# Elementwise work of the first feed-forward moved from GpSimd to VectorE, and the order of its queues changed

## The chip, the cores and the metric

The kernel runs on one core of a Trainium2 chip. The metric is the device time of one execution in microseconds; lower is better. The engines are TensorE (PE in the rows; its weight loads are PEld), VectorE (DVE), ScalarE (ACT), GpSimd (POOL) and SyncE (SP), whose queue issues the DMAs.

## The reference

Attention over 8 batches of 8 heads, 512 local and 32 global positions, heads of 64. A local query sees the global keys and the local keys at most 32 positions away; a global query sees all keys. The result, 4608 tokens of 512, goes through a feed-forward of 2048 with softplus between two products.

```python
s_g = scale * np.matmul(q_g, k_all.transpose(0, 1, 3, 2))
out_g = np.matmul(sm(s_g), v_all)
s_ll = np.where(np.abs(pos[:, None] - pos[None, :]) <= 32, scale * np.matmul(q_l, k_l.transpose(0, 1, 3, 2)), -1e9)
s_l = np.concatenate([scale * np.matmul(q_l, k_g.transpose(0, 1, 3, 2)), s_ll], axis=-1)
out_l = np.matmul(sm(s_l), np.concatenate([v_g, v_l], axis=2))
...
h = x @ w_in
g = np.maximum(h, 0.0) + np.log1p(np.exp(-np.abs(h)))
out = g @ w_out
```

## The kernel before

**The work.** Heads go in pairs: 32 pairs m, four to a batch, so that a pair fills the 128 partitions. The feed-forward takes one batch b at a time, its 512 local tokens, in 16 tiles f of 128 hidden units (a ninth, shorter round takes the global tokens). Each operand of its products is split into an upper half that TensorE takes at full rate and the rest: x into xh and xl, g into gh and gl, the weights into two halves of one tile. A product is then three matmuls (upper by upper, upper by rest, rest by upper), so h of a tile is 12 matmuls and its part of the output 12.

**Batch 0 (pairs 0 to 3)** is done first, in ten steps of a tight software pipeline (`scores0`, `invert0`, `diag0`, `turn0`, `evict0`, `values0`, `split0` and their global forms, whose names end in g). Here the order on VectorE and ScalarE is written out by hand: `keep("dve", ...)` and `keep("act", ...)` chain each instruction to the one before. `split0` casts the values into xh (ScalarE, L224) and subtracts for xl (VectorE, L226); `split0g` copies the global values into yg (L267). While this goes on, weight tiles are prepared, one to a step (`held`): `abs_w` (ScalarE, L479), four operations on bits in `bits_w` (VectorE, L486, L488, L489, L492), and `halves_w`, which copies the upper half (ScalarE, L497) and subtracts for the lower (GpSimd, L498). There are 32 weight tiles, in the order `order_w`; W_PRE = 12 of them are done in the steps.

**Pairs 4 to 31** go through pieces, each with a due time: scores of three parts p at 12 m + 4 p, values 22 (LAG) later, then `invert` and `normalise` 3 and 6 after the last values. Scores write PSUM (up to pair 7 the mask is added by TensorE, MPE = 8, and ScalarE copies the scores out; later VectorE adds the mask, L315), then a transposing reduction (L316) collects maxima of blocks of 32. After the third part, `maxima` (three copies across partitions on GpSimd, L329, then small reductions and copies on VectorE) and `probs` three times: a transpose spreads the maxima into mb (L347), GpSimd subtracts them (L352, L354, L355), ScalarE takes the exponential (L356). `values` multiplies into PSUM, ScalarE copies the result into x (L369, L373), and VectorE adds the overlapping columns (L374, L375). From pair 6 on, scores and values share one PSUM buffer, "a". `combine` sends the row sums through DRAM, `invert` takes the reciprocal and sends it back as rb, `normalise` multiplies (L404), and `split_x` splits the result for the next batch (L451, L452).

**The feed-forward's items** are half tiles of h (`hpart`) and, two tiles later, half tiles of the output (`opart`): 60 items in batch 0, each of 6 matmuls. After the second half of h comes `act`: Abs, Exp, Ln on ScalarE (L540 to L542), maximum and add on VectorE (e, L543, which frees the PSUM buffer of h; there are two), the cast gh on ScalarE (L546) and the subtraction gl on GpSimd (L547). After each item of batch 0 the weights are prepared up to W_AHEAD + w RATE / 8, where w is 4 f + 2 or 4 f + 4 from f = 1 on, and loaded AHEAD = 4 further; then all pieces go whose due time has come: from START at the first item to `first` + 48 = 120 at the last.

**Order.** TensorE's instructions run in the order in which the program emits them (`mm` chains each to the one before). For the other engines a planner lays out each queue ahead of time by when it expects instructions to be ready, and by emission among those that are ready; `after(i, what)` adds that i comes behind the last instruction noted under that name. So the bits of a weight behind the steps come after the latest maxima (L487). On the chip every queue runs in the order laid out.

Of the kernel before, what the change touches and what calls it, by code (L numbers as in the profile page):

```python
# [8 lines left out]
F32 = mybir.dt.float32  # L9
# [3 lines left out]
AF = mybir.ActivationFunctionType  # L13
ALU = mybir.AluOpType
# [18 lines left out]
LAG = 22  # L33
STEP = 3
GW = 75
W_AHEAD = 9
W_PRE = 12
START = 69
RATE = 4
A_LO = 8  # L40
A_UP = 5
# [12 lines left out]
def moe_over_global_local_attention(  # L54
# [271 lines left out]
    def maxima(m):  # L326
        mt = st.pop(("mt", m))
        for a in range(1, 4):
            nc.gpsimd.tensor_copy(mt[0:32, GW * a:GW * a + GW], mt[32 * a:32 * a + 32, 0:GW])  # L329
        e0 = 4 * GW  # L330
        for u, du, off in ((0, 1, -2), (3, 1, 3)):
            nc.vector.tensor_reduce(grid(mt, e0 + u, (7, 6), (du, 2)), grid(mt, 3 + u, (12, 6), (du, 2), (off, 2), (GW, 4)), axis=AX.XY, op=ALU.max)
        nc.vector.tensor_reduce(grid(mt, e0 + 2, (7, 6), (4, 2)), grid(mt, 3 + 2, (12, 6), (7, 2), (GW, 4)), axis=AX.X, op=ALU.max)
        g = e0 + 44
        nc.vector.tensor_reduce(grid(mt, g, (1, 2)), grid(mt, 3 + 5, (36, 2), (12, 3), (3, 2), (GW, 4)), axis=AX.XYZ, op=ALU.max)
        nc.vector.tensor_copy(grid(mt, e0 + 5, (21, 2), (7, 3)), mt[0:32, g:g + 2].unsqueeze(2).to_broadcast([32, 2, 3]))
        e = mt[:, e0:e0 + 44]
        for a in range(1, 4):
            i = nc.vector.tensor_copy(e[32 * a:32 * a + 32, 0:42], e[0:32, 0:42]).ins
        order["maxima"] = i  # L340
        st["e", m] = e

    def probs(m, p):
        s, e = st["s", m, p], st["e", m]
        k = QW[p] // 32
        mb = pl.tile([P, 2, 288], F32, tag="mb", name=f"mb{m}_{p}", bufs=2)
        nc.vector.transpose(mb[:, :, :QW[p]].rearrange("p h (s k) -> p h s k", k=32),  # L347
                            windows(e, 7 * p, 21, 2, k).unsqueeze(3).to_broadcast([P, 2, k, 32]))
        for h in range(2):
            if p < 2:  # L350
                sw = s[:, h].rearrange("p (c w) -> p c w", w=192)
                nc.gpsimd.tensor_tensor(sw, sw, windows(mb[:, h], 0, 96, 2, 192), op=ALU.subtract)  # L352
        if p == 2:
            nc.gpsimd.tensor_tensor(s[:, :, 0:192], s[:, :, 0:192], mb[:, :, 0:192], op=ALU.subtract)  # L354
            nc.gpsimd.tensor_tensor(s[:, :, 192:288], s[:, :, 192:288], mb[:, :, 96:192], op=ALU.subtract)  # L355
        nc.scalar.activation(s, s, AF.Exp, scale=0.125)  # L356

    def values(m, p):
        s, vt = st.pop(("s", m, p)), st["v", m]
# [51 lines left out]
    def pieces():  # L411
# [6 lines left out]
        for m in range(M0, M):  # L418
            for p in range(NPC):
                fs = [lambda m=m, p=p: scores(m, p)]  # L420
                if m + 1 < M:
                    fs.append(lambda m=m, p=p: load(m + 1, p))
                if p == 2:
                    fs.append(lambda m=m: maxima(m))
                    fs += [lambda m=m, q=q: probs(m, q) for q in range(NPC)]
                ps.append((12 * m + 4 * p, piece(*fs)))
                fs = [lambda m=m, p=p: values(m, p)]
                if p == 2:
                    fs.append(lambda m=m: combine(m))
                    if m + 2 < M:  # L430
                        fs.append(lambda m=m: load_v(m + 2))
                    ps.append((end(m) + STEP, lambda m=m: invert(m)))
                    ps.append((end(m) + 2 * STEP, lambda m=m: normalise(m)))
                ps.append((12 * m + 4 * p + LAG, piece(*fs)))
# [39 lines left out]
    def abs_w(kind, k):  # L474
        if A_LO <= k < NF - A_UP:
            a = pl.tile([P, 512], I32, tag=f"{kind}{k + A_UP}", name=f"wbits{kind}{k}", bufs=1)
        else:
            a = pl.tile([P, 512], I32, tag="mb", name=f"wbits{kind}{k}", bufs=2)
        note("act", nc.scalar.activation(a.bitcast(F32), raws[kind, k][:, :, 1].bitcast(F32), AF.Abs))  # L479
        return a  # L480

    def bits_w(kind, k, a):
# [1 line left out]
        lo32, hi32 = t[:, :, 0], t[:, :, 1]  # L484

        i = nc.vector.tensor_scalar(a.bitcast(F32), a.bitcast(F32), TINY, None, op0=ALU.max)  # L486
        note("dve", i) if tight else after(i, "maxima")  # L487
        note("dve", nc.vector.tensor_scalar(a, a, 3, 0x3FFFFFFF, op0=ALU.logical_shift_left, op1=ALU.bitwise_and))  # L488
        note("dve", nc.vector.scalar_tensor_tensor(a, hi32, -0x40000000, a, op0=ALU.bitwise_and, op1=ALU.bitwise_or))  # L489

# [4 lines left out]
    def halves_w(kind, k, r):  # L495
        (wi if kind == "wi" else wo)[k] = o = pl.tile([P, 2, 512], F32R, tag=f"{kind}{k}", name=f"{kind}{k}", bufs=1)
        note("act", nc.scalar.copy(o[:, 0], r))  # L497
        nc.gpsimd.tensor_tensor(o[:, 1], r, o[:, 0].bitcast(F32), op=ALU.subtract)  # L498

    def split_w(kind, k):  # L500
        halves_w(kind, k, bits_w(kind, k, abs_w(kind, k)))
# [10 lines left out]
    def moe_items():  # L512
# [24 lines left out]
        def act(b, f):  # L537
# [6 lines left out]
            gh = pl.tile([P, 512], F32R, tag="gh", name=f"gh{b}_{f}", bufs=3)  # L544
            gl = pl.tile([P, 512], F32R, tag="gl", name=f"gl{b}_{f}", bufs=3)
            nc.scalar.copy(gh, e)  # L546
            nc.gpsimd.tensor_tensor(gl, e, gh.bitcast(F32), op=ALU.subtract)  # L547
            g[b, f] = (gh, gl)

        def opart(b, f, t):  # L550
# [93 lines left out]
    for k in range(-2, n + 2):  # L644
        stage(k + 2, 0)

        while k >= n - 2 and pcs[0][0] < min(12 * M0 + 8 * (k - n + 3), START):
            pcs.pop(0)[1]()
        if k == 0:
            key_masks()  # L650
        if held:
# [7 lines left out]
        if held:  # L659
            halves_w(*held[:2], r)  # L660
            held = None
        if -1 <= k and wk[1] < W_PRE:
            held = order_w[wk[1]]
            held += (abs_w(*held),)
            wk[1] += 1
# [2 lines left out]
        halves_w(*held[:2], bits_w(*held))  # L668
    items = moe_items()
    loads(W_PRE + 6)  # L670
    weights(W_AHEAD)
    total = [sum(it[1] for it in items if it[0] == b) for b in range(B + 1)]
    gone = [0] * (B + 1)
# [70 lines left out]
```

## Time and profile before

| | |
|---|---|
| time, median of 3 runs | 1098.7 us (1097.0 to 1100.11) |
| the profiled execution | 1099.49 us |
| its span, first to last instruction | 1097.4 us |
| PE busy | 1037.4 us, 95% |
| VectorE busy | 599.2 us, 55% |
| ScalarE busy | 549.8 us, 50% |
| GpSimd busy | 466.7 us, 43% |
| mean granted TensorE clock | 0.977 |

Busy times are unions of the instructions of an engine. Shares over the span are means over stages that differ: batch 0's attention, the first feed-forward together with the preparation of weights, then seven feed-forwards with the attention of the pairs ahead beside them.

### The profile page before, as it was taken

How to read it: one execution, taken by the hardware profiler on the slowest of the kernel's cores; microseconds unless marked ns; L12 is line 12 of the kernel's file. 1: busy time of each engine (PE TensorE's matmuls, PEld its weight loads, DVE VectorE, ACT ScalarE, POOL GpSimd, SP SyncE). 2: the span in 40 equal slices, each digit the busy share in tenths (PEclk: the TensorE clock that was granted, in tenths of full speed). 3: DMA queues.
4: the chain of work that ended last, by engine and by line, in shares of the span. 5: the costliest groups of instructions: out<-in, count | busy, mean ns of one | idle time of the engine just before them, and what ended most of it. 6: DMA issues, size and time to landing. Idle time of an engine off the chain costs nothing.

```text
span 1097.4 us, 14272 instructions
## 1 busy us (share of the span) xinstructions
PE 1037.4 (95%) x5108; PEld 799.0 (73%) x5108; DVE 599.2 (55%) x1137; ACT 549.8 (50%) x972; POOL 466.7 (43%) x554
## 2 busy tenths in 40 slices
PE   6896788999999999999999999999999999999996
PEld 4674566767777777777777777777777778788895
DVE  5979697874445655565555544565546542311211
ACT  6855555544444544545444544554454544454452
POOL 2136475762345444454444344544445442222221
PEclk9997889999999999999999999999999999999998
DMA  9432332322112212123211312122212210110010
GB/s 359 157 98 86 108 129 64 94 53 84 50 49 49 89 44 55 47 54 93 55 48 52 93 44 55 48 81 53 55 45 55 84 28 13 32 39 1 1 39 20
DMA packets 78566, 74.14 MB, mean 68 GB/s; under 512 B 53380, under 2 KB 57476, under 8 KB 78496
## 3 DMA queue, kind: packets, MB, share of 16 engines
q1 hardware_dynamic: 77952, 73.17, 22.6%
q8 instruction: 40, 0.66, 0.2%
q14 instruction: 30, 0.25, 0.1%
q10 hardware_dynamic: 544, 0.07, 0.0%
HBM read 63.51 MB, written 9.71 MB: 67 GB/s over the span
## 4 chain that ended last, share of the span: by engine, by line
PE 74%; DVE 8%; DMA 4%; issue 3%; POOL 1%; ACT 1%; DVEq 0%; ACTq 0%; SPq 0%; POOLq 0%
PE h L124 30%; PE o L124 30%; PE v_ps L124 9%; PE s_ps L124 5%; DMA rb<-rec_scratch 3%; DVE xa L404 2%; DMA rec_scratch<-sc 1%; DVE xl L452 1%; DVE xh L451 1%; DVE s L315 1%; DVE mb L347 0%; DVE wbitswo L489 0%; DVE woraw L492 0%; DMA raw<-in_qk 0%; DVE wbitswo L486 0%
## 5 line engine op out<-in xcount | busy, mean ns | idle before, releaser
L124 PE MATMUL h<-xh,wi 128*128 128x512 f32 (+1 forms) x1152 | 357.9, 394 | 20.0 <-DVE xl L226 10.3
L124 PE MATMUL o<-wo,gh 128*128 128x512 f32 x1088 | 346.9, 400 | 0.0
L547 POOL TENSOR_TENSOR gl<-e,gh 128x512 fp32r<-128x512 f32 x136 | 178.5, 1313 | 378.9 <-ACT gh L546 322.7
L124 PEld LDWEIGHTS h<-xh,wi 128*128 128x128 f32 x1152 | 208.7, 190 | 69.7 <-issue 17.2
L124 PEld LDWEIGHTS o<-wo,gh 128*128 128x128 f32 x1088 | 201.4, 189 | 47.3 <-issue 4.0
L124 PE MATMUL h<-xl,wi 128*128 128x512 f32 (+1 forms) x576 | 221.1, 384 | 2.8 <-DVE xl L452 2.8
L540 ACT ACTIVATE e<-h 128x512 f32<-128x512 f32 x136 | 81.3, 598 | 272.3 <-PE h L124 265.5
L124 PE MATMUL o<-wo,gl 128*128 128x512 f32 x544 | 213.6, 393 | 0.0
L543 DVE SCALAR_TENSOR_TENSOR e<-h,e 128x512 f32<-128x512 f32 x136 | 93.2, 685 | 182.9 <-ACT e L542 182.9
L352 POOL TENSOR_TENSOR s<-s,mb 128x384 f32<-128x384 f32 x112 | 137.7, 1261 | 14.2 <-DVE mb L347 14.2
L124 PEld LDWEIGHTS h<-xl,wi 128*128 128x128 f32 x576 | 109.6, 190 | 27.7 <-DVE xl L452 5.8
L546 ACT CAST gh<-e 128x512 fp32r<-128x512 f32 x136 | 84.2, 619 | 90.0 <-DVE e L543 90.0
L124 PE MATMUL v_ps<-s,v 128*65 128x192 f32 (+1 forms) x672 | 126.3, 319 | 2.1 <-DVE s L315 1.8
L124 PEld LDWEIGHTS o<-wo,gl 128*128 128x128 f32 x544 | 103.0, 189 | 22.7
L124 PEld LDWEIGHTS v_ps<-s,v 128*65 128x65 f32 (+1 forms) x672 | 85.3, 136 | 41.5 <-issue 15.9
L315 DVE TENSOR_TENSOR s<-s_ps,mask 128x768 f32<-128x768 f32 (+1 forms) x96 | 64.7, 694 | 90.9 <-PE s_ps L124 90.9
L542 ACT ACTIVATE e<-e,one 128x512 f32<-128x512 f32 x136 | 98.5, 724 | 3.3
L356 ACT ACTIVATE s<-s 128x768 f32<-128x768 f32 (+1 forms) x84 | 66.6, 792 | 66.5 <-POOL s L352 51.4
L124 PE MATMUL s_ps<-raw 64*128 64x192 f32 (+1 forms) x672 | 81.8, 350 | 13.5 <-issue 9.4
L541 ACT ACTIVATE e<-e 128x512 f32<-128x512 f32 x136 | 85.6, 630 | 3.4
L124 PEld LDWEIGHTS s_ps<-raw 64*128 64x128 f32 (+1 forms) x672 | 50.2, 181 | 49.8 <-issue 41.3
L316 DVE TRANSPOSE_TENSOR_REDUCE mt<-s 128x24 f32<-128x768 f32 (+1 forms) x84 | 76.2, 908 | 13.4 <-ACT s L312 9.7
(144 smaller groups left out, 839.3 us busy)
## 6 DMA issues: line engine op xcount, KB each, us to landing
raw<-in_qk SPq DMA_DIRECT2D x56, 272.0 KB
v<-in_v SPq DMA_DIRECT2D x28, 384.0 KB
out<-ot SPq DMA_DIRECT2D x34, 256.0 KB
rb<-rec_scratch SPq DMA_DIRECT2D x28, 304.0 KB
wiraw<-in_w_in SPq DMA_DIRECT2D x16, 512.0 KB
woraw<-in_w_out SPq DMA_DIRECT2D x16, 512.0 KB
raw<-in_qk SPq DMA_DIRECT2D x28, 192.0 KB
v<-in_v SPq DMA_DIRECT2D x4, 512.0 KB
```

What stands on the lines that cost most here:

```text
L124: order["pe"] = after(nc.tensor.matmul(*a, **k), "pe").ins
L315: nc.vector.tensor_tensor(s[:n, :, o:o + w], ps[:n, :, o:o + w], mk[:n].unsqueeze(1).to_broadcast([n, 2, w]), op=ALU.add)
L316: order["scores"] = nc.vector.tensor_reduce(windows(mt, 3 + 12 * p, 36, 2, nb), s.rearrange("p h (b k) -> p h b k", k=32), axis=AX.X, op=A ...
L352: nc.gpsimd.tensor_tensor(sw, sw, windows(mb[:, h], 0, 96, 2, 192), op=ALU.subtract)
L356: nc.scalar.activation(s, s, AF.Exp, scale=0.125)
L404: after(nc.vector.tensor_tensor(y[64 * h:64 * h + 64], x[0:64, h], rb[:, h], op=ALU.mult), "scores")
L540: nc.scalar.activation(e, ph, AF.Abs)
L541: nc.scalar.activation(e, e, AF.Exp, scale=-1.0)
L542: nc.scalar.activation(e, e, AF.Ln, bias=one)
L543: nc.vector.scalar_tensor_tensor(e, ph, 0.0, e, op0=ALU.max, op1=ALU.add)
L546: nc.scalar.copy(gh, e)
L547: nc.gpsimd.tensor_tensor(gl, e, gh.bitcast(F32), op=ALU.subtract)
```

## The change

On VectorE instead of GpSimd, for as long as the first feed-forward lasts: the copies in `maxima` and the subtractions in `probs` of pairs 4 to 7 (m < MPE), the lower halves of weight tiles prepared after the steps, and gl of batch 0.

Order: maxima and probs of a pair become a piece of their own, due half a unit after its last scores, and in the steps only whole due times are taken, so those of pairs 4 and 5 are emitted behind all steps. The copies of `maxima` on VectorE and the first operation on bits come behind the last instruction of the steps on VectorE, the exponentials of `probs` and the Abs of later weights behind the last on ScalarE.

Pace: nine weight tiles instead of twelve are prepared in the steps (k from 0 to 8, not from -1 to 10); W_AHEAD is 12 instead of 9, so that three more are emitted straight behind the steps and the later ones three further ahead; START is 64 instead of 69.

```diff
-W_AHEAD = 9
+W_AHEAD = 12
...
-START = 69
+START = 64
...
     def maxima(m):
         mt = st.pop(("mt", m))
         for a in range(1, 4):
-            nc.gpsimd.tensor_copy(mt[0:32, GW * a:GW * a + GW], mt[32 * a:32 * a + 32, 0:GW])
+            if m < MPE:
+                after(nc.vector.tensor_copy(mt[0:32, GW * a:GW * a + GW], mt[32 * a:32 * a + 32, 0:GW]), "dve")
+            else:
+                nc.gpsimd.tensor_copy(mt[0:32, GW * a:GW * a + GW], mt[32 * a:32 * a + 32, 0:GW])
...
+        sub = nc.vector.tensor_tensor if m < MPE else nc.gpsimd.tensor_tensor
...
-                nc.gpsimd.tensor_tensor(sw, sw, windows(mb[:, h], 0, 96, 2, 192), op=ALU.subtract)
+                sub(sw, sw, windows(mb[:, h], 0, 96, 2, 192), op=ALU.subtract)
         if p == 2:
-            nc.gpsimd.tensor_tensor(s[:, :, 0:192], s[:, :, 0:192], mb[:, :, 0:192], op=ALU.subtract)
-            nc.gpsimd.tensor_tensor(s[:, :, 192:288], s[:, :, 192:288], mb[:, :, 96:192], op=ALU.subtract)
-        nc.scalar.activation(s, s, AF.Exp, scale=0.125)
+            sub(s[:, :, 0:192], s[:, :, 0:192], mb[:, :, 0:192], op=ALU.subtract)
+            sub(s[:, :, 192:288], s[:, :, 192:288], mb[:, :, 96:192], op=ALU.subtract)
+        after(nc.scalar.activation(s, s, AF.Exp, scale=0.125), "act")
...
+                ps.append((12 * m + 4 * p, piece(*fs)))
                 if p == 2:
-                    fs.append(lambda m=m: maxima(m))
-                    fs += [lambda m=m, q=q: probs(m, q) for q in range(NPC)]
-                ps.append((12 * m + 4 * p, piece(*fs)))
+                    fs = [lambda m=m: maxima(m)] + [lambda m=m, q=q: probs(m, q) for q in range(NPC)]
+                    ps.append((12 * m + 4 * p + 0.5, piece(*fs)))
...
-        note("act", nc.scalar.activation(a.bitcast(F32), raws[kind, k][:, :, 1].bitcast(F32), AF.Abs))
+        i = nc.scalar.activation(a.bitcast(F32), raws[kind, k][:, :, 1].bitcast(F32), AF.Abs)
+        note("act", i) if tight else after(i, "act")
...
-        note("dve", i) if tight else after(i, "maxima")
+        note("dve", i) if tight else after(after(i, "maxima"), "dve")
...
-        nc.gpsimd.tensor_tensor(o[:, 1], r, o[:, 0].bitcast(F32), op=ALU.subtract)
+        (nc.gpsimd if tight else nc.vector).tensor_tensor(o[:, 1], r, o[:, 0].bitcast(F32), op=ALU.subtract)
...
-            nc.gpsimd.tensor_tensor(gl, e, gh.bitcast(F32), op=ALU.subtract)
+            (nc.gpsimd if b else nc.vector).tensor_tensor(gl, e, gh.bitcast(F32), op=ALU.subtract)
...
-        while k >= n - 2 and pcs[0][0] < min(12 * M0 + 8 * (k - n + 3), START):
-            pcs.pop(0)[1]()
+        if k >= n - 2:
+            for pc in [pc for pc in pcs if pc[0] < min(12 * M0 + 8 * (k - n + 3), first - 2) and pc[0] % 1 == 0]:
+                pcs.remove(pc)
+                pc[1]()
...
-        if -1 <= k and wk[1] < W_PRE:
+        if 0 <= k < n - 1 and wk[1] < W_PRE:
...
     loads(W_PRE + 6)
+    while pcs[0][0] < first - 2:
+        pcs.pop(0)[1]()
     weights(W_AHEAD)
```

## Rows read from the trace of the kernel before

**Rows 1.** Busy us (instructions) of each engine by stretch, granted clock, DMA share, GB/s.

```profile
60.00:80.00 20.00, 20.00 (x149) 14.74 (x147) 16.64 (x34) 10.34 (x21) 6.80 (x10) 1.00 0.36 96
80.30:190.40 110.10, 84.14 (x382) 61.37 (x382) 89.78 (x142) 62.45 (x107) 66.26 (x66) 0.87 0.32 103
190.40:241.50 51.10, 49.21 (x233) 36.95 (x233) 40.55 (x75) 26.06 (x45) 31.26 (x35) 0.94 0.27 74
300.00:400.00 100.00, 98.60 (x483) 75.09 (x483) 59.62 (x114) 49.20 (x81) 49.37 (x60) 1.00 0.23 62
...
190.40:196.90 6.50, 6.41 (x20) 5.00 (x21) 6.43 (x11) 3.57 (x6) 3.17 (x3) 0.52 0.44 120
```

**Rows 2.** Waits of PE, 80 to 250 us: total us, times, longest.

```profile
PE h L124 <- DVE xl L226: 10.3, 1, 10.3
PE s_ps L124 <- issue: 9.4, 2, 6.1
PE s_ps L124 <- ACT wo L497: 4.1, 1, 4.1
PE h L124 <- DVE xh L451: 2.7, 1, 2.7
```

**Rows 3.** Timeline, 76 to 92 us: start us, us, instruction [idle before, releaser].

```profile
78.43 0.60 PE L124 MATMUL o<-p_1gl,v 96*128 96x256 f32 x2
...
83.81 0.72 ACT L224 CAST xh<-o 64x256 fp32r<-64x256 f32 x2
...
90.93 0.85 DVE L226 TENSOR_TENSOR xl<-o,xh 64x256 fp32r<-64x256 f32 x2
...
91.92 0.77 PE L124 MATMUL h<-xh,wi 128*128 128x512 f32 x1 [10.31 <-DVE xl L226]
```

**Rows 4.** Timeline around the second part of pair 8's scores.

```profile
190.18 0.21 DVE L375 TENSOR_TENSOR x<-x,v_ps 65x64 f32<-65x64 f32 x1
...
190.49 1.65 PE L124 MATMUL s_ps<-raw 64*128 64x192 f32 x8 [3.33 <-issue]
```

**Rows 5.** Timeline, 85 to 115 us: operations on weight bits, and a GpSimd subtraction.

```profile
101.53 0.42 DVE L486 TENSOR_SCALAR wbitswo<-wbitswo 128x512 f32<-128x512 f32 x1
...
101.99 0.43 DVE L488 TENSOR_SCALAR wbitswo<-wbitswo 128x512 int32<-128x512 int32 x1
...
104.92 1.50 POOL L547 TENSOR_TENSOR gl<-e,gh 128x512 fp32r<-128x512 f32 x1 [0.20 <-ACT gh L546]
...
105.19 1.52 DVE L486 TENSOR_SCALAR wbitswo<-wbitswo 128x512 f32<-128x512 f32 x1
```

**Rows 6.** Timeline, 12 to 20 us: the Abs of the first weight tile.

```profile
15.12 0.64 ACT L479 ACTIVATE wbitswi<-wiraw 128x512 f32<-128x512 f32 x1
```

**Rows 7.** Groups by line and form on VectorE, 262 to 900 us: busy us, mean ns.

```profile
L347 DVE STREAM_TRANSPOSE mb<-mt 128x576 f32<-128x576 f32 x44 | 31.7, 758 | 0.8
...
L452 DVE TENSOR_TENSOR xl<-xa,xh 128x384 fp32r<-128x384 f32 x10 | 5.3, 528 | 0.0
```

**Rows 8.** Chain that ended last, 260 to 290 us: start us, us, what.

```profile
272.76 2.75 PE h L124 x12
```

**Rows 9.** Busy us by stretch of tile wbitswo's instructions, then wbitswi's: VectorE, ScalarE.

```profile
80.30:190.40 110.10, 28.01 (x34) 5.98 (x9) 0.87 0.32 103
...
80.30:190.40 110.10, 30.73 (x35) 5.95 (x9) 0.87 0.32 103
```

**Rows 10.** Timeline of VectorE at 157 us: two independent operations in a row.

```profile
157.50 0.68 DVE L492 SCALAR_TENSOR_TENSOR wiraw<-wiraw,wbitswi 128x512 int32<-128x512 int32 x1
158.10 0.67 DVE L489 SCALAR_TENSOR_TENSOR wbitswi<-wiraw,wbitswi 128x512 int32<-128x512 int32 x1
```

**Rows 11.** Groups by line and form on GpSimd, 80.3 to 190.4 us.

```profile
L352 POOL TENSOR_TENSOR s<-s,mb 128x384 f32<-128x384 f32 x15 | 16.0, 1089 | 9.4 <-DVE mb L347 9.4
L547 POOL TENSOR_TENSOR gl<-e,gh 128x512 fp32r<-128x512 f32 x10 | 14.6, 1463 | 4.2 <-ACT gh L546 3.7 <-POOL mt L329 0.5
L498 POOL TENSOR_TENSOR wo<-woraw,wo 128x512 fp32r<-128x512 f32 x8 | 14.4, 1797 | 6.0 <-ACT wo L497 6.0
```

## The prediction, made before the changed kernel was run

> **What bounds the kernel now.** I read the windows first, then PE's waits, then the timeline at each wait. From 300 us on PE is busy 98.6 of 100 us, so nothing that this change touches can matter there; between 80.3 and 190.4 it is busy 84 of 110 at a granted clock of 0.87, and that is the stretch of the first feed-forward [rows 1]. Four waits hold most of its loss: 10.3 us in one piece before the first matmul of h, 9.4 in two pieces before scores, 4.1 before another, 2.7 at the change to the second batch [rows 2]. The first is a queue, not work: the last values of batch 0 leave PE at 79.0, but their cast to xh stands behind exponentials on ScalarE until 83.81, and xl, behind weight bits and maxima on VectorE, starts at 90.93 [rows 3]. The waits before scores are the single "a" bank: the scores at 190.49 start when the two small adds into x on VectorE (L374, L375) have emptied it, and these stood behind weight bits [rows 4]. PE's order is the emission order, so one late add stops all of PE. VectorE is thus what PE waits for, though it is busy only 89.8 of those 110 us [rows 1].
>
> Part of these 89.8 us is GpSimd's doing. Alone, two operations on weight bits took 0.42 and 0.43 us; with a GpSimd subtraction of 1.50 us beside it the first took 1.52 [rows 5].
>
> **The change, part by part.** Durations are of the profiled execution, whose own time is 1099.49 us over a span of 1097.4; the median of the runs is 0.8 lower, so I carry the difference over to 1098.7.
>
> *The start.* The first weight tile is taken out of the step at 15 us: its Abs (0.64 us on ScalarE [rows 6]) stood ahead of four exponentials, its bits ahead of the inversion that waits for them. Bounds: nothing, or all of it, 0.6 + 2.2 = 2.8. Without the tile VectorE would still wait for the exponentials, so what is gained is the Abs ahead of them and about as much of the bits as outlasted them; I take 1.2. Tiles 10 to 12 leave the tight steps too, but from 60 to 80 us PE is busy all 20 us [rows 1], so these buy nothing there. Their price comes later.
>
> *The first wait.* With maxima and exponentials of pairs 4 and 5 put behind the batch's last units, xh and xl follow the values at 79.0 at once: 0.7 and 0.85 us [rows 3], so h could start at about 80.3, or 79.1 with the start's gain: some 11 us earlier than 91.9. But what was put off is queued on VectorE ahead of the first softplus. By emission come maxima and subtractions of two pairs (an estimate: 2.6 us of subtractions and 0.6 of copies, worked out below, and 3.4 of reductions and transposes, of which a transpose of 576 takes 0.76 [rows 7]: 6.6 each) and three weight tiles at 2.7 (below): together 21. PE can do h of the first two tiles (two banks, 2.75 us for 12 matmuls [rows 8]), then stands until the softplus's add on VectorE (L543) at about 79 + 21 = 100. The wait of 10.3 is largely moved behind the second tile, and PE's granted clock will fall there as it did in the windows of the waits (0.52 from 190.4 to 196.9 [rows 1]). So the sum must be made on VectorE, at a place both versions pass: the second part of the scores of pair 8, due at 100 and at 190.5 us now. The old pace puts it after 37 of the 60 items of batch 0 (69 + 51 x 37/60 is over 100), the new ones after 39 (64 + 56 x 39/60).
>
> *VectorE's work up to that place.*
> - Now 89.8 us busy, of it 28.0 + 30.7 = 58.7 on weight bits, 69 operations, 17.25 tiles [rows 9]. The rest, 31.1, stays, less 0.9 for xl, which is now done before.
> - Bits: the new pace (12 ahead, not 9) puts tiles 10 to 31 ahead of this place: 22 tiles. Quiet they cost 0.42 + 0.43 + 0.68 + 0.68 less the overlap [rows 5, 10], 2.1 each: 46.2. At the present, disturbed mean (58.7/17.25 = 3.4) it would be 75; GpSimd has no such work left here until pair 8, so I take the quiet end.
> - Lower halves of these 22: on GpSimd 1.80 each for wo [rows 11]. VectorE's two-input operations of 512 columns start 0.60 apart (157.50, 158.10 [rows 10]): 13.2.
> - gl of ten tiles, 1.46 on GpSimd [rows 11]: 10 x 0.60 = 6.0.
> - Subtractions of pairs 4 to 7: 20 of 384 columns and 4 of 192. The nearest VectorE row is a subtraction of 384 columns in 0.528 [rows 7], less 0.06 overlap 0.47: 9.4 + 1.1 = 10.5, against 1.09 each on GpSimd [rows 11].
> - Twelve 32-partition copies at about 0.18: 2.2. Maxima and transposes of pair 4, now before 80 us: 3.3.
>
> Sum: 31.1 - 0.9 + 46.2 + 13.2 + 6.0 + 10.5 + 2.2 + 3.3 = 111.6 us, where 110 are there today. What contention gives back, the moved work takes. Of the 22 tiles the last three (8 us) are first used by tiles 13 and 14; the planner puts them ahead only where they are ready, and I let half stand behind: 107.6. Idle: today 20.3 us (110.1 less 89.8 [rows 1]); with some 20 us of work queued ahead I take 3 (bounds 0 and 20). The place is then passed at 79.1 + 107.6 + 3 = 189.7 instead of 190.5, with two items (2.75 us) more done.
>
> Here a rule of the Trainium skill speaks against the change: VectorE: DVE Perf Modes, section "The DRAIN you can't avoid", says that an operation is followed by a flush of about its duration less 266 ns in which the next cannot start. These rows do not bear it out: of independent operations lasting 0.68 the next started 0.60 after the first [rows 10]. By the rule each added subtraction would hold VectorE for 0.2 to 0.4 us more; by the rows, for nothing more.
>
> *The rest.* From 190.5 to the second batch's first h at 241.5 it is 51.0 us now, with PE busy 49.2 [rows 1]. VectorE has 40.6 of work there, of it almost five tiles of bits (22 less 17.25) that are then done, so PE sets the pace: less 2.75 for the two items, less half of the 3.1 us that the clock of 0.52 took from 6.5 us [rows 1] (the other half stays, since PE will have waited there again): 46.8. Batch 1 starts at 189.7 + 46.8 = 236.5 instead of 241.5, 5.0 earlier. At the change of batches the chain from the last values of pair 7 through the reciprocal to xh stays as long, but one item less (1.4 us) stands in front of its wait of 2.7 [rows 2]; half of that may come back from quieter multiplies: +0.8. Queues of SP: weight loads are issued earlier and past fewer loads of q and k, a gain where ScalarE waits for one, nothing otherwise. Total -4.2: **1094.5 us**.
>
> **The rivals.** *No change*: the same chain with 4 to 10 us idle on VectorE instead of 3; every microsecond idle before the place is one lost. For it: lower halves and gl wait for a ScalarE copy each. Against: other work is queued. 1095.5 to 1101.5, about 1098.
>
> *Slower*: VectorE becomes the bound and stays as poorly filled as now. Bits may not pass the latest maxima (L487), these wait for PE's scores, and PE waits for VectorE's adds into x, so a late VectorE starves itself. From 11 us idle (1102.5) it decides; with 17, near today's 20.3, the time is 14 more than in the sum: 1108.5. If each added operation held VectorE longer than the starts of rows 10 show, by 0.4 us at 512 columns and 0.2 at 384, 32 x 0.4 + 24 x 0.2 = 18 us would do it alone: 1112.5, with 2 in 100 inside this case. That is what the skill's rule on the flush, named above, would make of it.
>
> *Much faster*: the first of these adds slip into gaps ahead of the put-off work, PE runs from 82 us and VectorE is full. VectorE's total to the second batch (about 111.6 + 30) bounds it at 221, 20 before 241.5: 1079 to 1086. Against it: the put-off work is all emitted earlier and ready.
>
> *The change does nothing at the head*: xl stays behind other work. Only the tiles' chain is then ahead of it on VectorE, so I see no way and give 2 in 100, inside "slower".
>
> **How the numbers follow.** 3.3 us (0.3%) is about what a measurement of this kernel tells from no change. My forecast, faster by 3.3 to 12: 0.41; much faster: 0.07; no change: 0.26; slower: 0.26. The idle bounds (0 and 20) make 1091.5 and 1111.5, the undue tiles 4 more each way. For 8 in 10 I leave out the better half of "much faster" and the worst third of "slower": 1082 to 1107.
>
> **What would show it.** First h at 79 to 82 us, with no wait above 2 us before it; then a PE wait of over 8 us before the third tile's h, ended by VectorE's L543. Bits at 0.4 to 0.7 us each between 80 and 180, subtractions near 0.5 and 0.6 on VectorE. VectorE over 95% busy from 80 to 190, and scores of pair 8, part two, at 187 to 195. I am wrong if VectorE is busy below 90% there (slower), if PE has no long wait before the third h (much faster), or if the added operations start more than 0.65 us apart.

## The result, and the profile after

The changed kernel takes 1100.15 us (median of 20 runs), the kernel before 1097.5 (20 runs beside them): a ratio of 1.0019, 95% interval 1.0011 to 1.0026. That is slower by 2 us, within the 0.3% that were to count as no change, and 5.7 above the forecast of 1094.5. The profiled execution has a span of 1098.9 us.

This small difference is a sum of two large ones. The second batch's first h starts at 225.5 us, not at 241.5, so the first feed-forward is 16 us shorter, three times the gain that I forecast for it. Then, at the six changes of batches from there on, the changed kernel loses 17.8 us again, 2.5 at the first of them and 15.3 at the other five; 0.4 comes back at the end.

The windows of the part up to the second part of pair 8's scores, of the stretch of [rows 1], of the rest of the first feed-forward, and of the steady part:

```profile
79.30:168.50 89.20, 79.77 (x388) 58.86 (x386) 86.52 (x199) 61.54 (x105) 1.44 (x7) 0.98 0.37 122
...
80.30:190.40 110.10, 92.11 (x448) 67.64 (x446) 106.93 (x241) 70.64 (x120) 3.27 (x12) 0.96 0.35 111
168.50:225.50 57.00, 46.05 (x221) 34.35 (x220) 49.30 (x101) 27.71 (x47) 13.61 (x24) 0.88 0.24 66
300.00:400.00 100.00, 96.77 (x474) 73.26 (x473) 56.26 (x105) 48.08 (x80) 43.05 (x55) 1.00 0.22 59
```

VectorE (third pair of numbers) goes from 89.8 to 106.9 us of the 110, GpSimd (fifth) from 66.3 to 3.3, PE from 84.1 to 92.1. But from 300 to 400 us, where I had said that nothing could matter, PE is busy 96.8 and no longer 98.6.

PE's waits from 80 to 250 us, to be held against [rows 2]:

```profile
PE v_ps L124 <- issue: 13.1, 2, 10.9
PE h L124 <- DVE xh L456: 4.0, 1, 4.0
PE h L124 <- DVE e L549: 3.7, 1, 3.7
```

The wait of 10.3 us for xl is gone, and the waits before scores are nearly so. New are one of 10.9 us before values, at 182 us, and 3.7 us before the third tile's h. The timeline at the head, beside [rows 3]:

```profile
77.64 0.86 DVE L226 TENSOR_TENSOR xl<-o,xh 64x256 fp32r<-64x256 f32 x2 [1.14 <-ACT xh L224]
79.35 0.73 PE L124 MATMUL h<-xh,wi 128*128 128x512 f32 x2
...
88.06 0.69 DVE L549 SCALAR_TENSOR_TENSOR e<-h,e 128x512 f32<-128x512 f32 x1
...
88.81 1.20 PE L124 MATMUL h<-xh,wi 128*128 128x512 f32 x2 [3.71 <-DVE e L549]
```

The first h starts at 79.35 instead of 91.92. The first softplus add comes at 88.06, not at 100: the planner put it amid the put-off work and not behind it.

**Where it is lost.** PE's waits from 260 to 960 us are all at the changes of batches:

```profile
PE h L124 <- DVE xl L457: 8.1, 5, 1.6
PE h L124 <- DVE xh L456: 7.5, 5, 1.6
```

In the kernel before the same two sums are 2.0 and 5.1 us. The timeline of VectorE, GpSimd and PE at the change to the third batch shows why:

```profile
350.14 2.68 DVE L409 TENSOR_TENSOR xa<-x,rb 64x608 f32<-64x608 f32 x2
...
352.85 0.58 DVE L350 STREAM_TRANSPOSE mb<-mt 128x384 f32<-128x384 f32 x1
...
353.35 1.50 DVE L456 CAST xh<-xa 128x128 fp32r<-128x128 f32 x2
354.59 1.13 POOL L359 TENSOR_TENSOR s<-s,mb 128x384 f32<-128x384 f32 x1
...
354.77 1.10 DVE L457 TENSOR_TENSOR xl<-xa,xh 128x128 fp32r<-128x128 f32 x1
...
354.90 0.73 PE L124 MATMUL h<-xh,wi 128*128 128x512 f32 x2 [1.60 <-DVE xh L456]
...
355.79 0.94 DVE L315 TENSOR_TENSOR s<-s_ps,mask 128x768 f32<-128x768 f32 x1
...
356.66 0.54 DVE L457 TENSOR_TENSOR xl<-xa,xh 128x384 fp32r<-128x384 f32 x1
...
357.26 0.50 PE L124 MATMUL h<-xl,wi 128*128 128x512 f32 x1 [1.62 <-DVE xl L457]
```

Between the normalised xa and its split for the next batch stand the last transpose of another pair (0.58) and, between the two parts of xl, the mask add of the pair after it (0.94). In the kernel before the order is xa, xh, xh, xl, transpose, xl, mask add:

```profile
367.61 0.28 DVE L452 TENSOR_TENSOR xl<-xa,xh 128x128 fp32r<-128x128 f32 x1
367.81 0.57 DVE L347 STREAM_TRANSPOSE mb<-mt 128x384 f32<-128x384 f32 x1
368.31 0.51 DVE L452 TENSOR_TENSOR xl<-xa,xh 128x384 fp32r<-128x384 f32 x1
...
368.74 0.94 DVE L315 TENSOR_TENSOR s<-s_ps,mask 128x768 f32<-128x768 f32 x1
```

The transpose costs twice: with its result there, GpSimd goes on to the next subtraction at 354.59 without a gap, and xl of 128 columns, beside it, takes 1.10 us. It takes 1.09 to 1.10 us at all five changes, and 0.28 in the kernel before and in that of the first experiment (e1, below), where GpSimd is idle beside it. The Trainium skill, SBUF — State Buffer, section "Who interferes with whom", says that a VectorE operation with two SBUF inputs contends with a GpSimd operation that reads SBUF, and that the ports they share are an exclusive lock. The row agrees: the subtraction ends at 354.59 + 1.13 = 355.72, and xl behind it at 354.77 + 1.10 = 355.87.

At the four later changes the two waits are followed by a fall of the granted clock (the third number from the end), which about doubles their price:

```profile
467.00:478.00 11.00, 8.20 (x41) 5.81 (x39) 10.82 (x18) 3.55 (x5) 8.02 (x8) 1.00 0.18 56
478.00:481.00 3.00, 2.69 (x6) 2.15 (x7) 1.14 (x2) 1.89 (x4) 0.00 (x0) 0.50 0.00 0
```

Three microseconds at 1.2 instead of 2.4 GHz lose some 1.5. At the change to the third batch the clock stays at 1.00. By the starts of the same matmul in both traces, the change to the third batch costs 1.8 us more than before, and each of the next four 3.2 to 3.5.

What in the change reaches so far is one number: the due time 12 m + 4 p + 0.5 of maxima and exponentials holds for all pairs, not only for pairs 4 to 7. Beside e1, where this alone is undone, the changed kernel has VectorE's queue in the other order at these five changes, with a softplus add in another place, and on ScalarE an Abs behind an exponential instead of ahead of it; TensorE's, GpSimd's and SyncE's orders are the same. Ahead of the change to the third batch no queue's order differs between these two kernels, so the 2.5 us lost at the change to the second batch cannot be put down to the half step.

### The profile page after: what moved, and what is told of

Its sections match the earlier page's. It is cut to its first block, busy times and chain, and to the rows that moved or that the text cites. A ratio compares the mean times of both kernels' runs of the same rounds, so it can differ in the third digit from the quotient of the medians.

```text
span 1098.9 us, 14225 instructions
## 1 busy us (share of the span) xinstructions
PE 1038.8 (95%) x5108; PEld 800.4 (73%) x5108; DVE 609.3 (55%) x1212; ACT 550.3 (50%) x972; POOL 378.2 (34%) x479
## 4 chain that ended last, share of the span: by engine, by line
PE 74%; DVE 13%; DMA 6%; issue 3%; SPq 1%; ACT 1%; POOL 0%; DVEq 0%; ACTq 0%
PE o L124 30%; PE h L124 29%; PE v_ps L124 9%; PE s_ps L124 5%; DMA wiraw<-in_w_in 2%; DMA rb<-rec_scratch 2%; DVE xa L409 1%; DVE xl L457 1%; DMA raw<-in_qk 1%; DVE s L315 1%; DVE mb L350 1%; DVE mt L342 1%; DVE e L549 1%; DVE mt L316 1%; DMA rec_scratch<-sc 1%
## 5 line engine op out<-in xcount | busy, mean ns | idle before, releaser
L553 POOL TENSOR_TENSOR gl<-e,gh 128x512 fp32r<-128x512 f32 x120 | 154.6, 1288 | 389.2 <-ACT gh L552 333.5
L124 PEld LDWEIGHTS h<-xh,wi 128*128 128x128 f32 x1152 | 207.6, 189 | 64.4 <-DVE xh L456 14.6
L124 PE MATMUL v_ps<-s,v 128*65 128x192 f32 (+1 forms) x672 | 129.8, 326 | 14.8 <-issue 13.1
L124 PEld LDWEIGHTS v_ps<-s,v 128*65 128x65 f32 (+1 forms) x672 | 87.6, 140 | 55.8 <-issue 30.3
L357 POOL TENSOR_TENSOR s<-s,mb 128x384 f32<-128x384 f32 x96 | 119.9, 1279 | 23.0 <-DVE mb L350 23.0
L315 DVE TENSOR_TENSOR s<-s_ps,mask 128x768 f32<-128x768 f32 (+1 forms) x96 | 64.7, 694 | 90.7 <-PE s_ps L124 90.6
L379 DVE TENSOR_TENSOR x<-x,v_ps 65x128 f32<-65x128 f32 x56 | 15.8, 282 | 123.2 <-ACT x L378 123.1
L124 PE MATMUL s_ps<-raw 64*128 64x192 f32 (+1 forms) x672 | 79.5, 342 | 1.1 <-ACT e L547 0.9
```

The lines of the kernel that those rows point to most:

```text
L124: order["pe"] = after(nc.tensor.matmul(*a, **k), "pe").ins
L315: nc.vector.tensor_tensor(s[:n, :, o:o + w], ps[:n, :, o:o + w], mk[:n].unsqueeze(1).to_broadcast([n, 2, w]), op=ALU.add)
L357: sub(sw, sw, windows(mb[:, h], 0, 96, 2, 192), op=ALU.subtract)
L379: nc.vector.tensor_tensor(x[:, :, o:o + 64], x[:, :, o:o + 64], ps[0:65, :, 0:64], op=ALU.add)
L553: (nc.gpsimd if b else nc.vector).tensor_tensor(gl, e, gh.bitcast(F32), op=ALU.subtract)
```

## The experiments

All times of e1 to e16 are medians of four runs (e4: nine, one of them 5675.7 us). Ratios are to the kernel before, run beside them (1098.8 to 1099.7; beside the changed kernel 1097.5), with 95% intervals. "Second h" and "third h" are the starts of the first h of the second and third batch in the trace.

| kernel | us | ratio to before | second h | third h |
|---|---|---|---|---|
| before | 1098.7 | | 241.5 | 364.4 |
| changed | 1100.15 | 1.0011 to 1.0026 | 225.5 | 351.0 |
| e1: half step only for pairs 4 to 7 | 1084.2 | 0.9856 to 0.9886 | 225.5 | 348.2 |
| e2: before, half step for pairs 8 to 31 | 1115.3 | 1.0133 to 1.0183 | 241.0 | 364.1 |
| e3: e1, split of x first | 1078.9 | 0.9794 to 0.9835 | 225.4 | 345.1 |
| e4: e1, no work moved | 1095.8 | 0.9969 to 0.9990 | 238.4 | 361.5 |
| e5: e1, old order | 1083.7 | 0.9846 to 0.9876 | 221.2 | 348.9 |
| e6: e1, old pace | 1084.5 | 0.9848 to 0.9881 | 222.6 | 350.3 |
| e7: e3, last wi tile four places later | 1076.3 | 0.9772 to 0.9802 | 217.9 | 343.5 |
| e8: e3, last wi tile two places later | 1074.8 | 0.9761 to 0.9790 | 222.7 | 342.1 |
| e9: before, moved work only | 1084.7 | 0.9858 to 0.9891 | 223.0 | 347.8 |
| e10: e1, subtractions and copies back | 1075.7 | 0.9772 to 0.9801 | 217.1 | 341.2 |
| e11: e1, lower halves back | 1083.0 | 0.9844 to 0.9873 | 225.6 | 350.5 |
| e12: e1, gl back | 1085.9 | 0.9867 to 0.9896 | 226.7 | 351.2 |
| e13: changed, split of x first | 1080.6 | 0.9807 to 0.9839 | 225.4 | 344.4 |
| e14: e10, split of x first | 1067.7 | 0.9686 to 0.9723 | 217.1 | 336.2 |
| e15: e14, last wi tile two places later | 1070.3 | 0.9713 to 0.9752 | 217.7 | 336.8 |
| e16: e14, lower halves back | 1082.4 | 0.9822 to 0.9861 | 225.8 | 345.5 |

In the traces it is 731.0 to 734.7 us from the third h to the last instruction in every kernel but two: 747.9 in the changed kernel and 748.0 in e2, the two that have the half step in the later batches and nothing against it.

**e1, the half step taken from the later pairs.**

```diff
-                    ps.append((12 * m + 4 * p + 0.5, piece(*fs)))
+                    ps.append((12 * m + 4 * p + (0.5 if m < MPE else 0), piece(*fs)))
```

> The changed kernel, but the due time of maxima and exponentials is moved by half a step only for pairs 4 to 7, not for pairs 8 to 31; nothing else differs. Theory A: that half step makes the planner put a transpose and a mask add ahead of the last split of x on VectorE at each change of batches from the third batch on; each change then costs 1.8 us (the third batch) or 3.4 us (the later four) more than in the kernel before, 15.4 us in all. With it gone the lead of 16.0 us at the second batch's first h (225.5 instead of 241.5) should reach the end: 1100.1 - 15.4 = 1084.7, within 1082 and 1087, and VectorE's order at those five changes is that of the kernel before. Rival B: the end is held by something else than the first feed-forward (the loads, the last batch), and takes the lead back whatever stands at the changes: 1096 to 1100.

1084.2, and the lead of 16.0 us at the second h is 15.8 to 16.4 in all later batches. The five changes' waits are as in the kernel before, 5.0 and 2.0 us:

```profile
PE h L124 <- DVE xh L456: 5.0, 5, 1.1
PE h L124 <- DVE xl L457: 2.0, 5, 0.4
```

The timeline at its change to the third batch: the split stands ahead, but for one transpose, and xl takes 0.28.

```profile
350.48 1.10 DVE L456 CAST xh<-xa 128x128 fp32r<-128x128 f32 x2
351.51 0.28 DVE L457 TENSOR_TENSOR xl<-xa,xh 128x128 fp32r<-128x128 f32 x1
...
351.64 0.73 PE L124 MATMUL h<-xh,wi 128*128 128x512 f32 x2 [1.09 <-DVE xh L456]
351.71 0.56 DVE L350 STREAM_TRANSPOSE mb<-mt 128x384 f32<-128x384 f32 x1
352.21 0.51 DVE L457 TENSOR_TENSOR xl<-xa,xh 128x384 fp32r<-128x384 f32 x1
```

From 472 to 475 us, the stretch behind its next change, the clock stays at 1.00. Rival B falls.

**e2, the half step alone, put into the kernel before**, with the same half step for m from 8 on and none for pairs 4 to 7.

> The kernel before, with the half step for the maxima and exponentials of pairs 8 to 31 alone; the first feed-forward is as before. Theory A: the second batch's first h stays at 241.5, and the five later changes cost 1.8 + 4 x 3.4 = 15.4 us more: 1097.5 + 15.4 = 1112.9, within 1109 and 1116, with the granted clock at 0.5 for some 3 us behind the waits of the later four. Rival B: what the changed kernel loses later is the price of its earlier start: 1097.5, within 3.

1115.3, inside theory A's band, and the later changes have the waits of the changed kernel:

```profile
PE h L124 <- DVE xl L454: 8.1, 5, 1.6
PE h L124 <- DVE xh L453: 7.4, 5, 1.5
```

Behind them the clock falls to 0.5 at the first four of the five changes (at the last one it stays), where theory A had the later four; these four cost 3.3 to 3.5 us each, and the last 1.8. The loss comes without any earlier start; theory A is shown from both sides.

**e3, the split of x first**, by an order on VectorE: the last transpose of one pair and the mask add of the next come behind the last xl.

```diff
+        if m > MPE and m % 4 == 1 and p == 2:
+            after(i, "xl")        # i: the transpose
...
+                if m > MPE and m % 4 == 2 and p == 0:
+                    after(i, "xl")        # i: the mask add
...
+            if j == 3:
+                order["xl"] = i.ins
```

(The two are also emitted just behind split_x, due 0.1 later. The mask add takes its scores on TensorE with it: they run behind the first six matmuls of h instead of ahead of them, so that both starts in the table are 0.9 us earlier by that alone in e3, e7, e8 and e13 to e16.)

> The first of these kernels, and at each change of batches the last transpose of one pair and the mask add of the next are held behind the last split of x on VectorE (the first change too, where the changed kernel has PE wait 4.0 us for xh and 0.6 for xl). Theory A: the first change gains about 3 us, and the later ones lose what is left of the wait for xl (0.4 us): 1084.7 - 3 - 1 = 1080 to 1082. Rival: the held mask add makes the next scores' reduction late, and PE waits there instead: 1084 to 1087.

1078.9, 1.1 below theory A's band: the wait for xl is gone at all changes, and no scores wait.

**e13, the same order in the changed kernel itself**, half step and all (the edit is that of e3).

> The changed kernel with its half step for all pairs, and at each change of batches the last transpose of one pair and the mask add of the next held behind the last split of x on VectorE. Theory A1: what the half step costs are these two operations ahead of the splits and nothing else (not the softplus add that it puts between the reductions): 1078 to 1082, as the kernel without the half step and with the split first (1078.9). Rival A2: the reductions that come later with the half step make normalise and the split later too, and some 1 to 2 us stay lost at each of five changes: 1084 to 1090.

1080.6, as theory A1 has it: this order is worth 19.5 us in the changed kernel. By the traces 6.4 of them come at the change to the second batch, where the half step had moved nothing. That the loss at the other five lies in VectorE's order, and not in TensorE's, which this edit moves as well, rests on e1 and e2, where TensorE's order stays. PE's waits at the changes are 1.5 us each where they are about 1.0 in e3; that half microsecond is what is left of rival A2.

**e4, the work left on GpSimd.** Each of the four conditional choices of engine goes back to `nc.gpsimd`.

> The first of these kernels, but lower halves, gl, subtractions and copies across partitions of the first feed-forward stay on GpSimd: only the order and the pace are changed. Theory C: contention with GpSimd is what made VectorE's bits cost 3.4 us a tile instead of 1.9; without the move the 22 tiles that the new pace asks for cost 20 to 30 us more on VectorE than in the first of these kernels, less the 20 us of moved work that VectorE is spared, and the values and adds into x come late: second batch's first h at 230 to 242, total 1089 to 1101. Rival D: order and pace did it all, moving the work buys nothing: 225 and 1084.

1095.8, as theory C has it: without the move, order and pace give 3 of e1's 14.6 us. VectorE was as full as with the moved work, and did less. The windows from 79.3 to 179.8 us of e4 and of the changed kernel:

```profile
79.30:179.80 100.50, 79.76 (x368) 58.03 (x367) 96.62 (x144) 62.20 (x107) 65.99 (x63) 0.90 0.35 114
...
79.30:179.80 100.50, 91.07 (x444) 67.13 (x443) 97.81 (x221) 67.25 (x115) 2.00 (x9) 0.98 0.38 120
```

144 operations in 96.6 us, against 221 in 97.8 in the changed kernel, 57 of which are the moved work. One operation on weight bits in e4, busy us and mean ns:

```profile
L495 DVE SCALAR_TENSOR_TENSOR woraw<-woraw,wbitswo 128x512 int32<-128x512 int32 x11 | 14.8, 1346 | 0.1
```

The same operation in the changed kernel:

```profile
L498 DVE SCALAR_TENSOR_TENSOR woraw<-woraw,wbitswo 128x512 int32<-128x512 int32 x11 | 7.4, 676 | 0.0
```

**e5, the old order at the head**: no half step, and the chains to the steps' last instructions taken out.

```diff
-                    ps.append((12 * m + 4 * p + (0.5 if m < MPE else 0), piece(*fs)))
+                    ps.append((12 * m + 4 * p, piece(*fs)))
...
-        after(nc.scalar.activation(s, s, AF.Exp, scale=0.125), "act")
+        nc.scalar.activation(s, s, AF.Exp, scale=0.125)
```

(and so for the copies, the Abs and the bits)

> The first of these kernels (1084.2, second batch's first h at 225.5) without its order at the head: maxima and exponentials of pairs 4 to 7 are due with their scores again, and the four chains to the hand-written order are taken out; the moved work and the pace stay. Theory V (VectorE is full until pair 8, so what stands ahead of xl is only moved from behind the second tile of h to before the first): first h 4 to 8 us later than 79.3, the wait of 3.7 us at the third tile gone, second batch's first h at 225 to 229, total 1084 to 1088. Rival O: the order is where the lead comes from: the delay stays, 230 to 234, total 1089 to 1093.

**e6, the old pace**: W_AHEAD = 9, START = 69.

> The first of these kernels with the old pace: weights 9 tiles ahead of the items instead of 12, due times of the pieces from 69 instead of 64; order and moved work stay. Theory V: with GpSimd quiet VectorE has some slack, and the pace only shifts what stands in it; the late weights now meet the scores of pair 8 and 9: second batch's first h at 225 to 229, total 1084 to 1088. Rival P: pieces five steps later mean that values and adds of pair 7 come later, and the end of the chain to the second batch's xh with them: 230 to 235, total 1089 to 1094.

1083.7 and 1084.5: each equals e1. In e5 h starts 3.6 us later than in e1 and PE still waits 3.3 at the third tile; the first h of the second batch is earlier, but it then waits 5.6 us for the last xh, whose chain of reciprocal and product is no earlier. In both the second h (221.2 and 222.6) lies ahead of theory V's 225 to 229. Theory V as I wrote it holds in the total, not in these details.

**e9, the moved work alone**, in the kernel before.

> The kernel before with the moved work alone: copies across partitions, subtractions of pairs 4 to 7, lower halves of the later weight tiles and gl of the first feed-forward go to VectorE; order and pace stay as before. Theory V (moving the work is the whole gain; without order, and without pace, the time stayed at 1083.7 and 1084.5): 1082 to 1087. Rival S: order and pace can stand in for one another, and without both the head's wait of 10 us stays: 1089 to 1095.

1084.7. Although h starts only at 91.4, as before, after a wait of 9.8 us, the second h is at 223.0. So beside the moved work neither the order at the head nor the pace is needed: e1's whole gain comes with the moved work, and the wait of 10.3 us, with which my account of the kernel began, was no loss of its own there.

**e10 to e12, one part of the moved work back on GpSimd.**

> The first of these kernels (1084.2) with the subtractions and copies of pairs 4 to 7 on GpSimd again, lower halves and gl on VectorE. Of the 11.6 us that moving all of it gave (1095.8 against 1084.2), theory L (the loss goes with GpSimd's busy time beside VectorE, some 26 of 82 us here) gives 4 us of loss: 1086 to 1090. Rival T (VectorE has slack enough that one part alone is hidden): 1083 to 1085.5.

> The first of these kernels with the lower halves of the weights on GpSimd again (some 33 of 82 us there). Theory L: 5 us of loss, 1087 to 1091. Rival T: 1083 to 1085.5.

> The first of these kernels with gl of the first feed-forward on GpSimd again (some 23 of 82 us there). Theory L: 3 us of loss, 1086 to 1089. Rival T: 1083 to 1085.5; it could even be faster, for gl has time until the output's third matmul.

Neither theory holds for all three. The lower halves, back on GpSimd, change nothing (T), gl costs 1.7 us, between T's band and L's and with an interval that overlaps e1's, and the subtractions and copies make it 8.5 us *faster*, which neither had; yet all of it together costs 11.6. GpSimd's busy time is not the measure of the total. It does go with what the bits cost: from 79.3 to 179.8 us a tile of them keeps VectorE busy 2.1 us in the changed kernel (GpSimd busy 2.0 us), 2.4 in e12 (20.2), 2.3 in e10 (24.4), 2.6 in e11 (29.8), 2.9 in e16 below (59.8) and 3.3 in e4 (66.0). Nor is e11 equal by slack, as T has it: there TensorE is busy only 84.9 us of these 100.5 (90.7 in e1), and gets that back because the wait before values at 182 us (11.3 in e1) is not there. In e10 GpSimd is busy 24.5 us of the 100.5, and yet two of the four operations on a tile of wo are at 0.42 and two at 0.68:

```profile
79.30:179.80 100.50, 88.63 (x426) 65.77 (x425) 94.46 (x191) 68.20 (x117) 24.45 (x34) 0.95 0.37 119
```

```profile
L492 DVE SCALAR_TENSOR_TENSOR wbitswo<-woraw,wbitswo 128x512 int32<-128x512 int32 x11 | 7.5, 681 | 0.0
...
L489 DVE TENSOR_SCALAR wbitswo<-wbitswo 128x512 f32<-128x512 f32 x11 | 4.7, 423 | 2.7 <-ACT wbitswo L481 2.7
```

And what e10 mends is the new wait of 11 us at 182. In the changed kernel its chain is on the timeline:

```profile
175.84 0.79 SPq L470 DMA_DIRECT2D wiraw<-in_w_in  x1
...
180.72 0.67 ACT L484 ACTIVATE wbitswi<-wiraw 128x512 f32<-128x512 f32 x1 [1.97 <-DMA wiraw<-in_w_in]
...
185.91 0.67 DVE L498 SCALAR_TENSOR_TENSOR wlastwi<-wiraw,wbitswi 128x512 int32<-128x512 int32 x1
...
187.19 0.76 DVE L350 STREAM_TRANSPOSE mb<-mt 128x576 f32<-128x576 f32 x1
...
188.57 0.69 DVE L504 TENSOR_TENSOR wi<-wlastwi,wi 128x512 fp32r<-128x512 f32 x1
189.18 1.57 DVE L409 TENSOR_TENSOR xa<-x,rb 64x608 f32<-64x608 f32 x2
...
190.78 1.03 DVE L357 TENSOR_TENSOR s<-s,mb 128x384 f32<-128x384 f32 x2
...
192.79 1.52 PE L124 MATMUL v_ps<-s,v 128*65 128x192 f32 x4 [10.95 <-issue]
```

The load of the last tile of input weights is issued at 175.84 and its bits are done at 186.6. Pair 7's transpose, which shares two buffers (mb) with these bits, stands behind them on VectorE, its subtraction behind that tile's own lower half and a normalisation, and PE behind that.

**e7 and e8, that weight tile put off**, by four and by two places, with the split first.

```diff
-    order_w += [("wo", NF - 2)] + [None] * SPACE + [("wo", NF - 1)]
+    order_w.remove(("wi", NF - 1))
+    order_w += [None, ("wi", NF - 1), ("wo", NF - 2)] + [None] * SPACE + [("wo", NF - 1)]     # e8
```

> The kernel with the last split of x first (1078.9), and the last tile of the input weights is prepared beside the last of the output weights instead of four places earlier. Theory R: PE's wait of 11 us at 182 comes from the two buffers that the spread maxima of pair 7 share with the bits of late weights; the bits of the last input tile wait 4.9 us for their load, and pair 7's transposes, subtractions, exponentials and values queue behind them. With that tile behind, pair 7's transposes come ahead of the sums of pair 8 and the wait falls to below 5 us; the second batch starts 4 to 8 us earlier: 1071 to 1075. Rival: VectorE has no room there, and the tile's work (2.5 us and a load) only moves the wait to a later place, or PE then waits for the tile itself at h of tile 14: 1077 to 1081.

> As the one before, but the last tile of the input weights goes two places later instead of four, ahead of the last two output tiles. Theory R: the transposes of pair 7 come even earlier, and the tile is in time for h of tile 14: 1070 to 1075. Rival: as before, 1077 to 1081.

The wait falls to 3.9 us (e7) and 2.1 (e8), as theory R has it; of 7 to 9 us gained there 2.6 and 4.1 reach the end, e7 just short of R's band, e8 at its upper edge. In e7 PE waits 4.0 us for xh (1.8 in e3) and 1.1 for xl at the change of batches; in e8 two more waits for values, of 1.6 and 2.5 us, have come.

**e14 to e16, put together.**

> The kernel with the subtractions and copies of pairs 4 to 7 back on GpSimd (1075.7), with the split of x first at each change. Theory: the two gains are at different places (the wait of 11 us at 182, the changes from 220 us on) and add up: 1075.7 - 5.3 = 1070.4, within 1068 and 1073. Rival: the second batch's first h is held by the chain from pair 7's last values, which the split first does not shorten: 1074 to 1076.

> As the one before, with the last tile of the input weights two places later. Theory R (the wait at 182 comes from pair 7's subtractions standing behind late weight bits; with these subtractions on GpSimd that is already mended): no further gain, 1069 to 1073. Rival R2 (the shared buffers hold pair 7's transposes still): 3 to 5 us more: 1065 to 1068.

> The kernel with subtractions and copies back on GpSimd and the split first, with the lower halves on GpSimd as well, so that of the moved work only gl is on VectorE. Theory L: GpSimd is busy again for some 60 of 100 us and VectorE's bits go from 2.1 to 3 us a tile: 1077 to 1083. Rival: as with the halves alone, no loss: 1068 to 1073.

e14 takes 1067.7 us, 0.3 below the band forecast for it and 2.95% less than the kernel before (interval 2.8 to 3.1), and is the fastest of all: what moving gives without the subtractions, and the split of x first at each change. A later weight tile adds nothing there (e15): with the subtractions on GpSimd the place at 182 is mended. The lower halves, which made no difference beside the subtractions on VectorE (e11), cost 14.7 us beside the subtractions on GpSimd (e16, as theory L has it; 10.0 between the two traces), where VectorE's bits stretch again, GpSimd being busy 60 of 100 us:

```profile
79.30:179.80 100.50, 82.50 (x379) 60.42 (x379) 94.47 (x160) 64.33 (x110) 59.77 (x54) 0.92 0.35 111
```

So the parts don't add. I have not tried to explain each of them beyond that.

## Why the prediction failed

**The start** was sized at 1.2 us; h starts at 79.35, where I had 79.1. Right.

**The first wait.** Gone, as said. But "largely moved behind the second tile", to a stand until 100 us, is wrong: the wait is 3.7 us. I took the put-off work in its order of emission; the planner goes by readiness, and put the first softplus add after 9 us of it. The rival "much faster" had this mechanism, and I gave it 7 in 100. By e5 and e9 it mattered little, which fits VectorE's total being the limit, and for that reason the sum at the later place was the right one to make.

**VectorE's work up to the scores of pair 8** was put at 107.6 us, with 3 idle, and the place at 189.7. It is passed at 168.48 (pair 8's three parts are the scores at 158.72, 168.48 and 177.98, the first ones without mask products on TensorE), after 89.2 us with 86.5 busy:

```profile
168.48 0.92 PE L124 MATMUL s_ps<-raw 64*128 64x192 f32 x8
```

Idle is as taken (2.7); the work was sized 21 us too large. By emission 22 tiles stand ahead of the place; the planner, which goes by readiness, put the bits of 17 and the lower halves of 16 there:

```profile
79.30:168.50 89.20, 17.82 (x35) 5.91 (x9) 0.98 0.37 122
...
79.30:168.50 89.20, 17.18 (x33) 6.07 (x9) 0.98 0.37 122
```

(the first row is tile wbitswo, the second wbitswi; VectorE, then ScalarE). These 68 operations are busy 35.0 us, 2.1 a tile as I had it; from start to next start they took 31.3, where I had 46.2 less 4. In the same count the lower halves took 9.7 (13.2), subtractions with copies 9.4 (12.7), since pair 7's subtractions had not come by then, ten gl 6.0 (6.0), and all else 30.1 (33.5). So the count of what stands ahead was the wrong term. The mechanism, quiet bits in exchange for moved work, is the one that ran.

The rule on the flush as the prediction has it (the Trainium skill, VectorE: DVE Perf Modes, section "The DRAIN you can't avoid") is again not borne out: independent operations in a row start 0.60 apart and last 0.68. The section also says that a next operation that is not held starts earlier, which the prediction left out, and these rows fit that.

```profile
169.13 0.68 DVE L553 TENSOR_TENSOR gl<-e,gh 128x512 fp32r<-128x512 f32 x1
169.73 0.68 DVE L498 SCALAR_TENSOR_TENSOR woraw<-woraw,wbitswo 128x512 int32<-128x512 int32 x1
```

**The rest**, 46.8 us to the second batch, took 57.0: PE was busy 46.05 of it, and waited 10.9 at 182, which I had not foreseen. I had asked where a stall goes only for the first one; pair 7's subtractions, moved onto the queue that prepares the last weights, made this one. So the lead over the kernel before is 22.0 us at pair 8's scores and 16.0 at the second batch.

**The change to the second batch**, "+0.8" in my sum, came to 2.5 in the trace of the changed kernel, and to a gain of 0.2 in that of e1, though no queue's order differs between the two up to there. In the changed kernel the load of the reciprocals is issued 0.6 us later (222.34, in e1 221.71), the product xa takes 3.14 us instead of 2.45, and the granted clock from 225 to 240 us is 0.77 instead of 0.89. Why, I can't tell from one trace of each.

**The step that failed** is the opening claim: "From 300 us on PE is busy 98.6 of 100 us, so nothing that this change touches can matter there". A busy share of 98.6 speaks against a gain there, not against a loss. And the change does touch that part: the half step is written for every pair. It cost 15.3 us at the five changes of batches from the third batch on by the trace, and e1 and e2 show it from both sides (16.0 us back, 16.5 lost). In e1, where only that is undone, 16 us are gained at the second batch, where I had 5, and the time is 1084.2, inside "much faster".

That 1100.15 lies within 1082 to 1107, and next to "no change", is luck. The mechanism of that rival, 4 to 10 us idle on VectorE, did not run (2.7 idle); a gain three times the forecast met a loss that I had put at nothing.

How the half step comes to the other layout inside the planner I have not followed; that it does, in both kernels, and what the layout costs, is shown by e1, e2, e3 and e13.

## What to carry to other kernels

Read a diff for where its conditions do *not* stand: one number without its `if m < MPE` undid 16 us. A stretch in which an engine is busy 98% is not safe from a change but the place where a lost microsecond is paid once per round; look there at the one chain that has no slack, here normalise, split, next batch, and pin its order on the queue that it shares.

When work is moved off an engine to stop contention, move what meets the other engine's long runs, and not what stands on a chain that other engines wait for: the subtractions of pairs 4 to 7 did not belong on VectorE, and once they were off it, the lower halves did.

## What I had not expected of the hardware

Two waits of 1.5 and 1.6 us, 2 us apart, had 3 us at the lower clock behind them (478 to 481 us, 0.50); at the change to the third batch waits of 1.60 and 1.62 us left it at 1.00, while in e2 that change was followed by the fall and the last one was not. What decides it, these runs don't show. And a VectorE operation was four times as long for what another VectorE operation had released: xl of 128 columns took 1.10 instead of 0.28 us at each of five changes, because the transpose ahead of it had set GpSimd's subtraction off.
